# Linear attention, a token-and-channel mixer and a normalised channel mixer on one core: weight loads placed earlier, second weights decoded in the second mixing, and the last sums of the first mixing taken between the first products of the second

## The chip, the cores and the metric

The kernel runs on one core of one Trainium2 chip. The metric is device time in microseconds (us) of one execution. TensorE (PE) multiplies, VectorE (DVE), ScalarE (ACT) and GpSimd (POOL) do elementwise work, and SyncE (SP) issues almost all DMAs. Every engine takes its own instructions in order; SP's DMAs of this kernel all stand in one queue, and a DMA there that waits for a buffer holds those behind it.

## The reference

Three steps, in float32 from weights given as float64, B = 8 batches of S = 576 tokens, 512 channels:

```
q_s = exp(q - max_d q) / sum_d;   k_s = exp(k - max_s k) / sum_s        # 8 heads of 64
x   = q_s @ (k_s^T @ v)                                                 # linear attention
u   = x + (relu(x^T @ w_tok1) @ w_tok2)^T                               # token mixing, 576 -> 256 -> 576
x   = u + relu(u @ w_ch1) @ w_ch2                                       # first channel mixing, 512 -> 1536 -> 512
xn  = (x - mean) / sqrt(var + 1e-6) * g_ln
out = x + relu(xn @ w2_ch1) @ w2_ch2                                    # second channel mixing, 512 -> 2048 -> 512
```

## The kernel before

**Precision.** Each float32 operand of a matmul is a pair, a high part in the reduced format `fp32r` and the rest. Three matmuls (`PASSES`) make one product. ACT makes the high part and DVE or POOL the low one: `split`, and `relu_split` (L155 on ACT, L156 on DVE) for hidden values. A weight comes as 64 bits an element and is *decoded* by five operations (`decode`): rebias (L113 on ACT, or L111 on DVE where the decode is of the "late" form), shift (L119), sign (L126), low (L132 in the usual form), all DVE, and the splitting into parts (ACT L148 and POOL L150, or L140 and L141 in the late form).

**First channel mixing** (`Phase1`). The tokens are nine blocks of 512 columns; block 8 holds the leftover tokens of all batches. A block has twelve steps f. A step issues L1 (twelve 128x512 matmuls into `ph`, L707), the relu and split of the result into `h`, and L2 of the step two before (`LAG`; twelve 128x512 matmuls into four banks `acc`, L724). At a block's end `finish` adds the residual into `yT` (L745 on DVE, and L748 on POOL for the low part), `y_store` transposes `yT` (`py`, L659), takes the statistics (L670, L671) and stores rows. Work of other kinds is laid between the matmuls in two ways. `tick()` is called four times a step and runs what `later(n, ...)` put n ticks ahead. `work(7)` stands after L1 and after L2 and takes seven entries from a list `jobs`, so that a step takes fourteen.

**Preparing the second mixing**, in blocks 7 and 8. Its first product is done with Strassen-Winograd's seven products of 2x2 blocks. `combine_all` prepares the first weights (`w2_ch1`) in eight groups g: two loads of 512 KB into `stage` tiles (L835), decode, sums (L860), seven splits (ACT L886, POOL L891), three stores to `wc_dram` (L897). `w2_jobs` does the second weights (`w2_ch2`) in 16 chunks of 512 KB (load L1028): six of them into `stage` tiles in block 8, the other ten, in pairs, into parts of `yb` in the second mixing, decoded in the late form. `Root` computes the inverse deviation, turns it (`pm`, L794) and stores it. The normalised first tokens are made in place in `xs` by POOL's hats (L1098: subtract, multiply), ACT's gains, POOL's differences (L1113) and splits into seven operands `xc` (L1107, L1108).

**Second mixing.** Six sets of 768 tokens, eight passes q each (48 in all). A pass has seven products i (L1213, six 128x384 matmuls into one of two banks `pp`, in turn), each followed by `gather` (DVE L1226 and `relu_split`), and six `token_chunk`s of the pass before (L1251, six 128x512). `ring_load` (L1067) fetches the combined weights of pass q + 2 after products 3 and 6. `at(q, i, ...)` hangs work behind a product; `work(2)` takes two entries of `jobs` after each product from q = 1 on.

The order of all instructions is this written order; there is no scheduler. What the change moves is in `Combine.splitting`, `combine_all`, `w2_jobs`, `Root.start`, the loop over steps, the list of `at(...)` ahead of the passes, and `work` in the loop over passes.

## Time and profile before

| | |
|---|---|
| median of 3 runs | 1662.68 us (1662.41 to 1667.33) |
| the profiled execution | 1666.4 us |
| its span, first to last instruction | 1664.6 us |
| PE busy | 1599.8 us, 96% |
| DVE busy | 794.7 us, 48% |
| ACT busy | 494.6 us, 30% |
| POOL busy | 495.7 us, 30% |

The profile is of one execution, and 1.8 us of it lie outside the span. Busy times overlap; for a bound one asks which engine the others wait for, and where. A row of a timeline gives the start of a group of like instructions, how long the group took, the engine, the line of the kernel, the operation, output and inputs with their shapes, and in brackets the idle time before it with what ended it.

### The profile page before, as it was taken

Reading aid. Unit: us, or ns where it says so; the run is one execution under the profiler, and the core shown is the slowest. Engines: PE = TensorE matmul, PEld = TensorE weight load, DVE = VectorE, ACT = ScalarE, POOL = GpSimd, SP = SyncE. Lnnn points to the kernel's source line nnn. Section 1 sums busy time; section 2 is a strip of 40 time slices with the busy share of each in tenths; the row PEclk is TensorE's granted clock in tenths of the full one; section 3 lists DMA queues with packets and bytes.
Section 4 is the critical chain, followed back from the end, with each engine's and each line's share of the span. In section 5 each row is a group of like instructions: output and inputs, shape, how many; then the busy total and the mean of one; then the engine's idle time right before and its main releaser. Section 6 shows DMA issues by size and latency. Waiting matters only on the chain. (4 is left out here: it accounts for less than half of the span.)

```text
span 1664.6 us, 21709 instructions
## 1 busy us (share of the span) xinstructions
PE 1599.8 (96%) x8241; PEld 1401.3 (84%) x8241; DVE 794.7 (48%) x1551; ACT 494.6 (30%) x1022; POOL 495.7 (30%) x412
## 2 busy tenths in 40 slices
PE   5999999999999999999878899999999999999998
PEld 4888888888888888877757789889889989998997
DVE  7775535344443435355645555335335335335333
ACT  5663323333232323333332223122122122122111
POOL 5744612232222314233652350320320320320001
PEclk8999999999999999999989999999999999999999
DMA  8552313122121313047754545544544544544341
GB/s 218 143 164 81 116 41 95 43 78 58 42 88 38 99 35 94 22 165 272 295 204 153 178 169 186 173 167 146 173 168 145 171 171 143 173 171 139 121 171 38
DMA packets 154398, 222.58 MB, mean 134 GB/s; under 512 B 97918, under 2 KB 114102, under 8 KB 146102
## 3 DMA queue, kind: packets, MB, share of 16 engines
q1 hardware_dynamic: 145750, 202.02, 37.9%
q10 hardware_dynamic: 5600, 9.73, 1.6%
q0 software_dynamic: 2944, 9.44, 1.6%
q8 instruction: 65, 1.06, 0.3%
q14 instruction: 39, 0.32, 0.1%
HBM read 174.98 MB, written 46.17 MB: 133 GB/s over the span
## 5 line engine op out<-in xcount | busy, mean ns | idle before, releaser
L1213 PE MATMUL pp<-xc,wr 128*128 128x384 f32 x2016 | 398.2, 340 | 15.3 <-DVE h L156 8.0
L1213 PEld LDWEIGHTS pp<-xc,wr 128*128 128x128 f32 x2016 | 362.6, 189 | 36.5 <-DVE h L156 9.5
L707 PE MATMUL ph<-u,w 128*128 128x512 f32 x1296 | 327.3, 398 | 11.3 <-DVE h L156 11.3
L724 PE MATMUL acc<-h,w 128*128 128x512 f32 x1296 | 329.0, 399 | 4.6 <-DVE yT L745 4.6
L1251 PE MATMUL acc<-w,h 128*128 128x512 f32 x1152 | 289.8, 393 | 0.0
L707 PEld LDWEIGHTS ph<-u,w 128*128 128x128 f32 x1296 | 238.7, 190 | 59.8 <-DVE h L156 12.2
L724 PEld LDWEIGHTS acc<-h,w 128*128 128x128 f32 x1296 | 240.9, 191 | 53.5 <-ACT wc L886 5.0
L1251 PEld LDWEIGHTS acc<-w,h 128*128 128x128 f32 x1152 | 214.4, 188 | 38.8
L155 ACT ACTIVATE h<-sc 128x384 fp32r<-128x384 f32 x144 | 75.6, 525 | 329.5 <-DVE sc L1226 327.0
L1251 PE MATMUL acca<-w,h 128*128 128x512 f32 x576 | 148.3, 394 | 0.0
L156 DVE SCALAR_TENSOR_TENSOR h<-ph,h 128x512 fp32r<-128x512 f32 x108 | 74.0, 686 | 144.8 <-ACT h L155 144.5
L156 DVE SCALAR_TENSOR_TENSOR h<-sc,h 128x384 fp32r<-128x384 f32 x144 | 90.1, 626 | 94.3 <-ACT h L155 94.3
L1098 POOL TENSOR_TENSOR xs<-xs 128x768 f32<-128x768 f32 x48 | 89.4, 1887 | 144.8 <-DMA xs<-mr_dram 144.8
L1267 POOL DMA_DIRECT2D out<-yb x32 | 17.7, 553 | 361.3 <-DVE yb L1263 361.2
L1251 PEld LDWEIGHTS acca<-w,h 128*128 128x128 f32 x576 | 107.8, 189 | 16.7
L1226 DVE TENSOR_TENSOR sc<-su,pp 128x384 f32<-128x384 f32 x144 | 79.5, 552 | 60.8 <-PE pp L1213 59.9
L155 ACT ACTIVATE h<-ph 128x512 fp32r<-128x512 f32 x108 | 64.2, 594 | 142.3 <-PE ph L707 140.9
L1226 DVE TENSOR_TENSOR su<-su,pp 128x384 f32<-128x384 f32 x96 | 53.0, 552 | 104.3 <-PE pp L1213 104.1
L486 POOL TENSOR_TENSOR qt<-rawq,qm 128x640 f32<-128x640 f32 x24 | 30.3, 1261 | 228.3 <-PE pt L480 130.6
L156 DVE SCALAR_TENSOR_TENSOR h<-pp,h 128x384 fp32r<-128x384 f32 x48 | 26.7, 556 | 144.1 <-ACT h L155 144.1
L155 ACT ACTIVATE h<-pp 128x384 fp32r<-128x384 f32 x48 | 23.6, 491 | 241.6 <-PE pp L1213 241.6
L629 PE MATMUL pu<-w,hs 128*128 128x288 f32 x384 | 61.8, 296 | 0.1
(178 smaller groups left out, 1740.5 us busy)
## 6 DMA issues: line engine op xcount, KB each, us to landing
wr<-wc_dram SPq DMA_DIRECT2D x48, 1024.0 KB, 5.1
wr<-wc_dram SPq DMA_DIRECT2D x48, 768.0 KB, 4.4
st<-in_moe_w_ch SPq DMA_DIRECT2D x23, 512.0 KB, 4.8
yT_dram<-yT SPq DMA_DIRECT2D x9, 1024.0 KB, 5.0
vt<-in_v SPq DMA_DIRECT2D x64, 128.0 KB, 3.1
y_dram<-yn ACTq DMA_DIRECT2D x32, 256.0 KB, 2.6
wc_dram<-wc SPq DMA_DIRECT2D x16, 512.0 KB, 3.2
out<-yb POOLq DMA_DIRECT2D x32, 256.0 KB, 2.8
```

The source lines that it names most:

```text
L155: nc.scalar.activation(out=hi, in_=x, func=AF.Relu)
L156: nc.vector.scalar_tensor_tensor(out=lo, in0=x, scalar=0.0, in1=hi.bitcast(F32), op0=ALU.max, op1=ALU.subtract)
L486: nc.gpsimd.tensor_tensor(out=self.qt, in0=self.qr.rearrange("p h c d -> p c h d"), in1=self.qm.unsqueeze(3).to_broadcast([P, NC + 1, 2, D ...
L629: nc.tensor.matmul(out=pu[:, 0:HN], lhsT=l, rhs=r, start=(n == 0), stop=(n == len(terms) - 1))
L707: nc.tensor.matmul(out=ps, lhsT=w[:, x, kk, fo:fo + P], rhs=u[:, y, kk], start=(n == 0), stop=(n == 3 * KD - 1),)
L724: nc.tensor.matmul(out=self.acc[dd], lhsT=w[:, x, f % 2, dd * P:(dd + 1) * P], rhs=h[:, y], start=(f == self.f0 and n == 0), stop=(f == se ...
L1098: nc.gpsimd.tensor_tensor(out=y, in0=y, in1=m, op=(ALU.subtract, ALU.mult)[op])
L1213: nc.tensor.matmul(out=bank[(BANK[i] + q) % 2][:, 0:HT], lhsT=r[:, x, kk], rhs=xc[i][:, y, kk], start=(n == 0 and not add), stop=(n == 5), ...
L1226: nc.vector.tensor_tensor(out=o, in0=x, in1=y, op=ALU.add)
L1251: nc.tensor.matmul(out=acc[c], lhsT=h[:, x, m * P:(m + 1) * P], rhs=wb2[p][:, y, f], start=(p == 0 and n == 0), stop=(p == NP - 1 and n == 5),
L1267: nc.gpsimd.dma_start(out=dst, in_=y)
```

## The change

- In `Combine.splitting` the three splits that need no sum come first. `combine_all` loads the first two groups at once, waits 20 empty entries, and issues the load of group g + 1 among the splits of group g - 1, at the sixth place. Splits and decoding alternate one to one.
- `Root` turns and stores two and three ticks later.
- `w2_jobs` goes by single chunks with a `depth` of loads ahead and a `gap` of empty entries. Only chunks 0 and 1 are done in block 8. Chunks 2 and 3 are loaded into the upper half of `xs` behind the first product and decoded in the late form; chunks 4 to 15 go through four parts of `yb` from product (1,1) on, with three loads ahead. `work` takes two entries a product in pass 0 and three afterwards.
- The four ring loads of passes 0 and 1 are spread over ticks 6 to 18 of step 6.
- The last step of block 8 does no L2. The three L2s that are left stand after products 0 and 1 and, in halves, after 3 and 4; the sums into `yT` follow product 4, POOL's additions products 5 to 8, and the `y_store`s the first four of pass 1. The tiles that are taken over (`acc`, `yb`, `acca`, `h11`) are taken later by as much.

```diff
-            for n, fn in zip((0, 2, 6, 8), (self.root, self.rstd, self.turn, self.store)):
+            for n, fn in zip((0, 2, 8, 11), (self.root, self.rstd, self.turn, self.store)):
...
-            ops += part(A11, 0) + part(s[:, 0], 1) + part(A12, 2) + [store(0, 3)]
+            ops += part(A11, 0) + part(A12, 2) + part(A22, 6)
+            ops += part(s[:, 0], 1) + [store(0, 3)]
             ops += part(s[:, 1:3], 3, 2) + [store(3, 2)]
-            ops += part(s[:, 3], 5) + part(A22, 6) + [store(5, 2)]
+            ops += part(s[:, 3], 5) + [store(5, 2)]
...
+                if 0 < g < NP - 1:
+                    f.insert(6, cs[g + 1].load)
                 ops = []
                 while f or d[:-4]:
-                    ops += f[0:2]
-                    del f[0:2]
+                    if f:
+                        ops.append(f.pop(0))
                     if len(d) > 4:
                         ops.append(d.pop(0))
-                ops += [cs[g + 1].load] if g + 1 < NP else []
...
-            jobs.extend(todo + [lambda: expand(0)])
+            jobs.extend([cs[0].load, cs[1].load] + [nop] * 20 + [lambda: expand(0)])
...
+        def w2_jobs(chunks, stages, depth, ts=None, gap=12):
...
+                if not ts:
+                    ops = [ops[0], lambda x=ops: [x[k]() for k in (1, 2, 3)], nop, ops[4]]
+                jobs[0:0] = ops
+
+            out = [lambda n=n: load(n) for n in chunks[:depth]] + [nop] * gap
+            for k, n in enumerate(chunks):
+                out.append(lambda n=n: go(n))
+                if k + depth < len(chunks):
+                    m = chunks[k + depth]
+                    out.append(lambda m=m: load(m))
             return out
...
-                    later(8, lambda: [ring_load(n, x) for n in range(2) for x in range(2)])
+                    later(6, lambda: ring_load(0, 0))
+                    later(9, lambda: ring_load(0, 1))
+                    later(14, lambda: ring_load(1, 0))
+                    later(18, lambda: ring_load(1, 1))
...
-                    jobs += w2_jobs(range(0, 3), lambda i: stage(512))
+                    jobs += w2_jobs([0, 1], lambda n: stage(512), 2)
...
-            if len(pend) > LAG:
+            if len(pend) > LAG and not (o.j == B and f == NF1 - 1):
                 do_L2()
...
         def last_rows():
+            do_L2(nop, range(2, KD))
             tmp["add"] = lastp.finish()
...
-        at(0, 0, lambda: do_L2(nop))
+        at(0, 0, lambda: jobs.extend(w2_jobs([2, 3], flat64, 2, ts, 6)))
...
+        at(0, 0, lambda: [do_L2(nop), h_tile(("11", 0))])
         at(0, 1, lambda: do_L2(nop))
-        at(0, 2, last_rows)
+        at(0, 2, lambda: h_tile("22"))
+        at(0, 3, lambda: pend[0][0].L2(*pend[0][1:], nop, range(2)))
+        at(0, 4, last_rows)
+        for c, (q, i) in enumerate(((0, 5), (0, 6), (1, 0), (1, 1))):
+            at(q, i, lambda c=c: tmp["add"](c))
+        at(1, 1, lambda: nc.sync.dma_start(out=yT_dram[B], in_=yT_t[B]))
         for c in range(CT):
-            at(0, 3 + c, lambda c=c: tmp["add"](c))
-        at(0, 6, lambda: nc.sync.dma_start(out=yT_dram[B], in_=yT_t[B]))
-        for c, (q, i) in enumerate(((0, 5), (0, 6), (1, 0), (1, 1))):
-            at(q, i, lambda c=c: y_store(B, c))
+            at(1, c, lambda c=c: y_store(B, c))
...
+            jobs.extend(w2_jobs([*range(4, NF2)], flat64, 3, ts, 0))
...
-        at(0, 6, take_over)
-        at(1, 1, more_acc)
+        at(0, 6, take_banks)
+        at(1, 1, take_over)
+        at(1, 3, more_acc)
+        at(2, 6, other_h)
...
-                if q and jobs:
-                    work(2)
+                work(2 + (q > 0))
```

How instructions stand on SP's queue while the weights are combined (loads L835 into the tiles `st` and `stage`, stores L897 of a group's results), before:

```order
L835 DMA st<-in_moe_w_ch 128x2x512 x2
L835 DMA stage_6662<-in_moe_w_ch 128x2x512
L835 DMA stage_6663<-in_moe_w_ch 128x2x512
L897 DMA wc_dram<-wc 128x1536
L897 DMA wc_dram<-wc 128x1024 x2
```

and after:

```order
L835 DMA stage_6662<-in_moe_w_ch 128x2x512
L835 DMA stage_6663<-in_moe_w_ch 128x2x512
L754 DMA yT_dram<-yT 128x2048
L835 DMA st<-in_moe_w_ch 128x2x512 x2
L897 DMA wc_dram<-wc 128x1536
```

The loads of the third group have moved ahead of the first group's stores, and so on for the later groups.

SP's queue from the end of block 8 to the second pass (L1028 chunks of the second weights, L1067 ring loads `wr`, L1300 the last store of `yT`), before:

```order
L1028 DMA st<-in_moe_w_ch 128x1024 x3
L1067 DMA wr<-wc_dram 128x2048
L1067 DMA wr<-wc_dram 128x1536
L1067 DMA wr<-wc_dram 128x2048
L1067 DMA wr<-wc_dram 128x1536
L1028 DMA st<-in_moe_w_ch 128x1024 x3
L1067 DMA wr<-wc_dram 128x2048
L1300 DMA yT_dram<-yT 128x2048
L1067 DMA wr<-wc_dram 128x1536
L1028 DMA yb<-in_moe_w_ch 128x1024 x2
```

and after (the same, as L1027, L1057 and L1305):

```order
L1027 DMA st<-in_moe_w_ch 128x1024 x2
L1057 DMA wr<-wc_dram 128x2048
L1057 DMA wr<-wc_dram 128x1536
L1057 DMA wr<-wc_dram 128x2048
L1057 DMA wr<-wc_dram 128x1536
L1027 DMA xs<-in_moe_w_ch 128x1024 x2
L1057 DMA wr<-wc_dram 128x2048
L1057 DMA wr<-wc_dram 128x1536
L1305 DMA yT_dram<-yT 128x2048
L1027 DMA yb<-in_moe_w_ch 128x1024 x3
```

Two chunk loads instead of three stand ahead of the four ring loads and two instead of three behind them, now into `xs`; the first loads into `yb` are three and stand behind the store of `yT`, as before.

DVE's queue in the first seven products (L1226 and L1220 the gathers, L745 the last sums of the first mixing, L111 to L126 the decode of a chunk), before:

```order
L156 SCALAR_TENSOR_TENSOR h_7874<-pp,h_7874 128x384
L745 TENSOR_TENSOR yT<-acc_7391,u 128x512
L745 TENSOR_TENSOR yT<-acc_7392,u 128x512
L745 TENSOR_TENSOR yT<-acc_7393,u 128x512
L745 TENSOR_TENSOR yT<-acc_7394,u 128x512
L1226 TENSOR_TENSOR su<-su,pp 128x384
L1226 TENSOR_TENSOR sc<-su,pp 128x384
L156 SCALAR_TENSOR_TENSOR h_7928<-sc,h_7928 128x384
```

and after:

```order
L1220 TENSOR_TENSOR sc<-su,pp 128x384
L156 SCALAR_TENSOR_TENSOR hh<-sc,hh 128x384
L745 TENSOR_TENSOR yT<-acc_7367,u 128x512
L745 TENSOR_TENSOR yT<-acc_7368,u 128x512
L745 TENSOR_TENSOR yT<-acc_7369,u 128x512
L745 TENSOR_TENSOR yT<-acc_7370,u 128x512
L111 TENSOR_SCALAR xs<-xs 128x512
L1220 TENSOR_TENSOR sc<-su,pp 128x384
L156 SCALAR_TENSOR_TENSOR h_7825<-sc,h_7825 128x384
L119 TENSOR_SCALAR sd<-xs 128x512
```

The four sums stood behind the third product's gather and now stand behind the fifth's, with the first operation of chunk 2 after them and ahead of the sixth's.

## Rows read from the trace of the kernel before

**Rows 1.** The page's forty slices: TensorE's busy share, in tenths.

```profile
PE   5999999999999999999878899999999999999998
```

**Rows 2.** Windows: stretch, length, busy PE, PEld, DVE, ACT, POOL; clock; DMA.

```profile
744.63:810.37 65.74, 56.98 (x234) 46.00 (x233) 39.92 (x71) 25.30 (x56) 27.12 (x32) 0.92 0.76 280
847.70:886.96 39.26, 25.63 (x97) 20.31 (x96) 20.10 (x24) 14.78 (x24) 19.38 (x11) 0.83 0.38 148
886.96:909.31 22.35, 20.19 (x101) 18.00 (x100) 12.78 (x26) 5.22 (x10) 5.68 (x4) 0.92 0.63 223
922.87:933.66 10.79, 5.60 (x20) 4.80 (x19) 6.73 (x12) 0.73 (x2) 5.53 (x3) 0.68 0.49 182
938.19:942.89 4.70, 2.69 (x13) 2.08 (x13) 3.98 (x5) 1.10 (x3) 2.81 (x2) 1.00 0.96 338
962.40:971.28 8.88, 5.24 (x20) 4.64 (x20) 7.57 (x11) 1.61 (x3) 4.38 (x3) 0.81 0.14 33
984.85:1000.53 15.68, 15.68 (x80) 14.13 (x78) 8.09 (x12) 3.60 (x7) 10.74 (x6) 1.00 0.35 118
```

**Rows 3.** PE's timeline where nothing waits: start, length, engine, line, operation, names.

```profile
718.70 2.88 PE L707 MATMUL ph<-u,w 128*128 128x512 f32 x12
721.42 2.88 PE L724 MATMUL acc<-h,w 128*128 128x512 f32 x12
...
988.33 1.21 PE L1213 MATMUL pp<-xc,wr 128*128 128x384 f32 x6
989.38 1.54 PE L1251 MATMUL acca<-w,h 128*128 128x512 f32 x6
```

**Rows 4.** PE's timeline, two waits in A and B.

```profile
805.12 5.46 PE L724 MATMUL acc<-h,w 128*128 128x512 f32 x12 [4.58 <-DVE yT L745]
...
867.63 4.99 PE L707 MATMUL ph<-u,w 128*128 128x512 f32 x12 [9.94 <-DVE h L156]
```

**Rows 5.** ACT's timeline: the first step of a decode, in A and B.

```profile
745.02 0.66 ACT L113 ACTIVATE st<-st 128x512 f32<-128x512 f32 x1 [5.20 <-DMA st<-in_moe_w_ch]
...
861.76 0.65 ACT L113 ACTIVATE st<-st 128x512 f32<-128x512 f32 x1 [9.89 <-DMA st<-in_moe_w_ch]
```

**Rows 6.** SP's timeline in B.

```profile
848.02 1.82 SPq L1067 DMA_DIRECT2D wr<-wc_dram  x4
...
850.51 16.58 SPq L1028 DMA_DIRECT2D st<-in_moe_w_ch  x3
```

**Rows 7.** POOL's groups, 815 to 990: count, busy us, mean ns, idle before.

```profile
L1098 POOL TENSOR_TENSOR xs<-xs 128x768 f32<-128x768 f32 x16 | 30.0, 1892 | 30.6 <-DMA xs<-mr_dram 30.6
...
L1113 POOL TENSOR_TENSOR xs<-xs 128x768 f32<-128x768 f32 x4 | 8.7, 2165 | 0.2
L150 POOL TENSOR_TENSOR w<-st,w 128x512 fp32r<-128x512 f32 x6 | 7.8, 1306 | 13.2 <-ACT w L148 13.2
```

**Rows 8.** DVE's timeline in C, D, E and F.

```profile
889.21 2.47 DVE L745 TENSOR_TENSOR yT<-acc,u 128x512 f32<-128x512 f32 x4
...
925.92 0.90 DVE L111 TENSOR_SCALAR yb<-yb 128x512 f32<-128x512 f32 x1 [7.44 <-DMA yb<-in_moe_w_ch]
...
939.29 1.74 DVE L786 TENSOR_SCALAR r<-r 128x8 f32<-128x8 f32 x1
...
942.99 0.43 DVE L111 TENSOR_SCALAR yb<-yb 128x512 f32<-128x512 f32 x1
...
962.06 1.84 DVE L111 TENSOR_SCALAR yb<-yb 128x512 f32<-128x512 f32 x1 [5.03 <-DMA yb<-in_moe_w_ch]
```

**Rows 9.** DMA issues, 740 to 980: count, KB each, median us to landing.

```profile
st<-in_moe_w_ch SPq DMA_DIRECT2D x11, 512.0 KB, 4.9
...
yb<-in_moe_w_ch SPq DMA_DIRECT2D x10, 512.0 KB, 8.4
```

**Rows 10.** Window of the tile `yb` alone (ten decodes): busy DVE, ACT, POOL.

```profile
900.00:990.00 90.00, 25.29 (x40) 5.99 (x10) 13.65 (x10) 0.94 0.57 198
```

**Rows 11.** SP's waits over the whole span: total us, times, longest.

```profile
SPq L1067 <- PE pp L1213: 665.3, 91, 22.1
```

More of the change, by code (lines that the diff above doesn't have):

```diff
@@ L712, in L1, with L2 @@
             return ps, BLK
-        def L2(self, f, h, mid):
-            if f == self.f0:
+        def L2(self, f, h, mid, dds):
+            if f == self.f0 and not dds[0]:
                 self.acc = [
@@ L719, in L2 @@
             w = wb[f // 2]
-            for dd in range(KD):
+            for dd in dds:
                 if dd == KD // 2:
@@ L977, with do_L2 @@
             steps += [(o, f) for f in range(o.f0, o.f1)]
-        def do_L2(mid=tick):
+        def do_L2(mid=tick, dds=range(KD)):
             o, f, h = pend.pop(0)
@@ L996, in combine_all @@
             cs = [Combine(g) for g in range(NP)]
-            todo = [cs[0].load]
-            late = []
             def expand(g):
@@ L1014, in expand @@
                 jobs[0:0] = ops
-            jobs.extend(todo + [lambda: expand(0)])
-        def w2_job(g, stages, ts=None):
-            box = {}
-            def load(i):
-                def fn():
-                    if i == 0:
-                        wb2[g] = main.tile([P, 2, 2, DM], F32R, tag="w", bufs=NF1, name="w")
-                    st = box[i] = stages(i)
-                    f0 = (2 * g + i) * P
-                    nc.sync.dma_start(
-                        out=st.rearrange("p d t -> p (d t)"), in_=w2_ch2[f0:f0 + P, :]
-                    )
-                return fn
-            def go():
-                both = [
-                    decode(box[i], lambda x: x, wb2[g][:, 0, i], wb2[g][:, 1, i], ts and ts[i])
-                    for i in range(2)
-                ]
-                if ts:
-                    jobs[0:0] = [x for pair in zip(*both) for x in pair]
-                    return
-                ops = [b[0] for b in both]
-                for b in both:
-                    ops += [lambda b=b: [b[n]() for n in (1, 2, 3)], nop, nop]
-                jobs[0:0] = ops + [b[4] for b in both]
-            return [load(0), load(1)], go
@@ L1048, in w2_jobs, with load, go @@
-        def w2_jobs(gs, stages, ts=None):
-            made = [w2_job(g, stages, ts) for g in gs]
-            out = list(made[0][0])
-            for n, (_, go) in enumerate(made):
-                out.append(go)
-                if n + 1 < len(made):
-                    out += made[n + 1][0]
+            jobs.extend([cs[0].load, cs[1].load] + [nop] * 20 + [lambda: expand(0)])
+        def w2_jobs(chunks, stages, depth, ts=None, gap=12):
+            st = {}
+            def load(n):
+                g, i = n // 2, n % 2
+                if i == 0:
+                    wb2[g] = main.tile([P, 2, 2, DM], F32R, tag="w", bufs=NF1, name="w")
+                st[n] = stages(n)
+                nc.sync.dma_start(
+                    out=st[n].rearrange("p d t -> p (d t)"), in_=w2_ch2[n * P:(n + 1) * P, :]
+                )
+            def go(n):
+                ops = decode(
+                    st[n], lambda x: x, wb2[n // 2][:, 0, n % 2], wb2[n // 2][:, 1, n % 2],
+                    ts and ts[n % 2],
+                )
+                if not ts:
[7 more added lines that the diff above has]
+                    out.append(lambda m=m: load(m))
@@ L1294, with flat64 @@
         lastp = steps[-1][0]
-        at(0, 0, lambda: do_L2(nop))
-        at(0, 1, lambda: do_L2(nop))
-        at(0, 2, last_rows)
+        sts = [xs[0][:, i * 1024:(i + 1) * 1024] for i in (2, 3)]
+        ts = [sd[:, i * 512:(i + 1) * 512].bitcast(U32) for i in range(2)]
+        at(0, 0, lambda: jobs.extend(w2_jobs([2, 3], flat64, 2, ts, 6)))
+        def flat64(n):
+            return sts[n % len(sts)].bitcast(U32).rearrange("p (n t) -> p n t", t=2)
+        at(0, 0, lambda: [do_L2(nop), h_tile(("11", 0))])
@@ L1301, with take_banks @@
[L1301 to L1302 removed]
+            at(1, c, lambda c=c: y_store(B, c))
+        def take_banks():
+            for i, c in enumerate((3, 4, 5, 0)):
+                acc[c] = ps_acc.tile([P, 512], F32, tag=f"acc{i}", name=f"acc{i}")
         def take_over():
[L1305 to L1324 removed]
@@ L1326, in more_acc @@
+            y = main.tile([P, 4096], F32, tag="u", bufs=2, name="yb")
+            yb.append(y)
+            tmp["t2"] = y[:, CS * DM:CS * DM + 2 * HT].rearrange("p (k n) -> p k n", k=2)
+            sts[:] = [y[:, i * 1024:(i + 1) * 1024] for i in range(4)]
+            jobs.extend(w2_jobs([*range(4, NF2)], flat64, 3, ts, 0))
         def more_acc():
```

32 lines of the change are left out of this document (8 added, 24 removed).

## The prediction

> **What bounds the kernel now.** I read four kinds of view, from coarse to fine. First the forty slices of the page [rows 1]: TensorE (PE) is busy nine tenths and more of almost every slice; only the first one, the last one and four about the middle (the 20th to the 23rd, 791 to 957 us) are lower. So the span is PE's own work nearly everywhere, and a change that takes nothing off PE can gain only where PE waits. Next the stretches of that dip, as PE's waits cut them [rows 2]; I call them A to F in the order of those rows, and the last row is a steady pass of the second mixing. Then PE's timeline at full rate [rows 3]: twelve 128x512 matmuls follow one another after 721.42 - 718.70 = 2.72 us, six 128x384 after 989.38 - 988.33 = 1.05 us; so six of 512 columns are 1.36. A lone small product of 128 columns I put at 0.09, an estimate from 2.72/12 = 0.227 for 512 columns with its hand-over.
>
> With these each stretch has a full-rate length, and what is above it is loss (waits, and the lower granted clock that follows them):
> - A, 228 matmuls of 512 = 19 x 2.72 = 51.7, some six small ones 0.4: 52.1 of 65.74, loss 13.6.
> - B, 7 x 2.72 + 2 x 1.05 = 21.1 of 39.26, loss 18.1.
> - C, ten products 10.5, four token chunks 5.4, sixteen transposes 1.4: 17.3 of 22.35, loss 5.0.
> - D and F, each two products and one token chunk, 3.5: of 10.79 and 8.88, losses 7.3 and 5.4.
> - E, one product and one chunk, 2.4 of 4.70, loss 2.3.
>
> Together 51.7 us, 3.1% of the span. The granted clock stood at 0.68 to 0.92 of full speed in A to D and F, at 1.00 in E and the steady pass [rows 2].
>
> Who is late there: in A and B the chain begins at DMA. ScalarE (ACT) is in order; its L113, the first step of decoding a weight, waited 5.20 us for a load, and 9.89 in the worst place [rows 5]. Behind it in ACT's queue stand the relus (L155) without which VectorE (DVE) cannot finish `h`, and PE stood 9.94 us for `h` [rows 4]. The 9.89 has its reason on SP: four ring loads were issued at 848.02, the third to fifth chunk from 850.51 behind them [rows 6]. In D and F it is DVE's own L111 that waits for chunks in `yb`, 7.44 and 5.03 us [rows 8], with the gathers behind it.
>
> **The change part by part.** No matmul is added or removed, so each part is costed as what is left of the losses.
>
> *Combining loads (A).* Seventeen entries of `jobs` instead of seven now lie between a load and its first use. Fourteen entries go with one step of two groups, 5.44 us, so ten more are 3.9 us: a lead of about 6.6 against a landing of 4.9 [rows 9]. ACT should stop waiting; the cover is 1.7 us and a load that lands late gives the difference back. The stall of 4.58 on `yT` [rows 4] came as DVE stood behind ACT, so it should go as well. The transpose `pm` is two ticks later, hence after `mr`. The twenty empty entries put the combining 20/14 = 1.4 steps later; the jobs of chunks 0 and 1 stand behind it in the same list, so that they can only come later. Left: 1 (0 to 5; the upper end if half the landings still outrun the lead).
>
> *End of block 8 (B).* The two remaining chunk loads stand ahead of all ring loads on SP, and these are spread over twelve ticks: the cause of the 9.89 is gone. What is late next is GpSimd (POOL). It has still, in its order, the last group's splits, four hats of 1.89, two chunk splits of 1.31 and four diffs of 2.17 [rows 7]; and the chunk loads stand in SP's queue behind the last store of combined weights, which waits for POOL's last split of a group. Chain from there: landing 4.9, two decodes at the 2.53 of the nearest row [rows 10] 5.1, two splits 2.6, four diffs 8.7 and one hat between them 1.9 come to 23.2; PE has 7 x 2.72 + 1.05 = 20.1 of work before it needs the last operand, so it is some 3 late, and 4 with the clock. Left: 4 (1 to 10; the ends are the whole chain hidden, and chunk loads that land after 8.4 as `yb`'s do [rows 9], plus a hat).
>
> *First seven products (C).* The pending L2s of 9, 10 and 11 now fill gaps between products, the same 36 matmuls. DVE's four last sums L745 (2.47 together, [rows 8]) and L111 now stand ahead of the gathers of products five and six; PE has two banks, so the product of the next pass waits for most of that: 2 to 3 us. The new late decode of chunks 2 and 3 is on DVE here too, 2 x 2.5 us [rows 10]. Its loads have the span of three products and two L2s, 8.6 us, against 4.9 to 8.4. Left: 4.5 (2 to 7).
>
> *Chunk 4 onward (D).* Its load cannot start before POOL's last addition L748, since the buffer is the old `u`; it stands behind the store of `yT` on SP, and the decode follows one product later in `jobs`. From the first product of the stage: three L2s and five products 13.4, sums 2.5, four additions at POOL's 1.31 for tiles of that size [rows 7] 5.2, landing 8.4: 29.5 us. DVE gets there with the tenth product, by PE's rate and C's loss after 27 to 28. It waits some 2, the rest is clock. Left: 4 (1 to 8; the upper end is the old wait).
>
> *Rstd (E).* L784 to L786 are still issued while POOL does hats: 1.74 us for 128x8 [rows 8]. Left: 2 (0 to 4).
>
> *Later chunks (F).* The loads stand three ahead; one chunk is taken up in 7 entries, three per pass, so the lead is about 15 us against 8.4. But SP is one queue: a chunk load stands behind ring loads that wait for products (665.3 us in 91 waits, 7.3 each, the longest 22.1 [rows 11]) and the x load. Left: 2 (0 to 6).
>
> *Denser decode (G), new.* Twelve chunks instead of ten lie in the second mixing, and three per pass rather than two: 3 x 2.53 = 7.6 us of DVE per pass [rows 10] on top of the 8.09 of a steady pass, 15.7 of 15.68 at worst [rows 2], though a part of the 2.53 is itself time beside POOL. Before, the fewer chunks lost nothing outside D to F. Left: 4 (0 to 10; the ends are decode wholly in gaps and each of twelve chunks giving back 0.8 us).
>
> Sum: 1 + 4 + 4.5 + 4 + 2 + 2 + 4 = 21.5 left of 51.7, a gain of 30.2. The profiled execution, 1666.4 around a span of 1664.6, would be 1636; it is 0.2% above the median of the runs, 1662.68, and from that the forecast is 1662.7 - 30.2 = **1632.5 us**, with 1624 to 1643 for it alone (every term half a step off).
>
> **A rule against this change.** L111 took 0.43 us at 942.99 and 1.84 at 962.06 while a hat of POOL's ran; the 128x8 operation of E took 1.74, also beside a hat [rows 8]. The Trainium skill, SBUF — State Buffer, section "SBUF: two separate sides", says that the port pair that VectorE and GpSimd share is an exclusive lock: an instruction of either that needs it holds it to its end, and the other is fully blocked. The trace agrees in that the excess of L111, 1.4 us, is under one hat. By that rule more decoding on DVE while POOL has hats, subtractions and diffs makes each collision cost up to a POOL instruction, and the gain would be smaller; that is the second rival, which I work out from the rows.
>
> **The rivals.**
> 1. *Nearly every stall goes* (A 0, B 2, C 2, D 2, the rest 1 each): 9 left, gain 42.7, **1620**. For it: each named wait is on a load, and each load is earlier. [...]
> 2. *DVE becomes the bound in passes one to four*: twelve chunks that each meet a hat or a subtraction lose 1.4, some 17 us; as gatherings stand behind them PE sees most: G 10, D 8, E 4, F 5, with A, B and C as forecast 36.5 left, gain 15, **1647**. For it: 7.6 + 8.09 fills a pass. Against: DVE's queue may run ahead into the two banks' slack.
> 3. *The change doesn't do what it says*: the landings stretch as more loads are in flight, ACT's L113 waits on as before (A 13.6, B 10), the rest as forecast: 40 left, gain 12, **1651**. For it: the 4.9 is a median, and `yb`'s 8.4 shows what traffic does.
> 4. *Slower*: SP's queue. Chunk loads 7 to 15 are issued with no lead, because ring loads ahead of them wait for products, and DVE's L111 waits a whole landing, 8.4, for each of nine chunks: 75.6 instead of F's 2. That is 44 above before, **1706**. It decides from a mean wait of 30.2/9 + 0.2 = 3.6 us per chunk. For it: the longest wait of 22.1 is more than a lead of 15. Against: these loads stand between ring loads whose products are near.
>
> **How the numbers follow.** Chances: forecast 0.57, first rival 0.13, second 0.13, third 0.07, slower by SP's queue 0.05, and 0.05 for several of these in part that end within 0.3% (5 us, about what a measurement of this kernel can tell from no change). Faster is 0.57 + 0.13 + 0.13 + 0.07 = 0.90, same 0.05, slower 0.05. The range takes in the forecast and the second rival, 1618 to 1652; it leaves out the better half of the first rival, the two last cases and a little of the third, some 0.2.
>
> **What would show it.** Right: no L113 of 3 us or more on DMA in blocks 7 and 8; no gap near 10 before L707 at the end of block 8, and a late POOL diff as the releaser of what is left; the first product of the second pass released by DVE behind L745; one L111 wait of 2 to 3 us for chunk 4 and none after; steady passes of 15.7. Wrong: L113 waits that stay (third rival); L111 or L119 of 1.5 us and more all through passes one to four with PE released by DVE (second); repeated L111 waits on `yb` loads (fourth); or a loss in a stretch that lost nothing before.

## The result, and the profile after

The changed kernel takes **1647.05 us** (median of 4 runs, 1645.75 to 1647.95). Against the kernel before, run beside it (1664.92), the ratio is 0.9892 with a 95% interval of 0.9871 to 0.9913: about 18 us faster. The forecast was 1632.5, so the sign and the range held, and little more than half of the forecast gain came. The profiled execution has a span of 1645.5 us against 1664.6, 19.1 less.

The page's forty slices of the kernel after, TensorE's busy share in tenths (it answers [rows 1]):

```profile
PE   5999999999999999999998799999999999999998
```

Of the four low slices two are left, 864 to 946 us. Windows of the kernel after, in the order of [rows 2] and with the same columns: from a step of block 8 to product (0,5), the next eleven products, then old D, old E, the stretch between, old F:

```profile
836.33:867.16 30.83, 26.79 (x115) 21.99 (x114) 17.49 (x18) 11.55 (x19) 14.39 (x8) 0.94 0.51 195
867.16:898.93 31.77, 27.25 (x137) 23.21 (x136) 25.55 (x45) 8.35 (x16) 9.96 (x8) 1.00 0.59 205
898.93:904.84 5.91, 5.91 (x31) 5.41 (x30) 4.22 (x6) 1.34 (x3) 2.15 (x2) 1.00 0.87 335
904.84:924.77 19.93, 13.30 (x49) 11.07 (x48) 15.99 (x23) 3.62 (x7) 10.23 (x6) 0.83 0.57 200
924.77:933.11 8.34, 8.34 (x44) 7.59 (x42) 5.68 (x10) 3.16 (x6) 1.29 (x1) 1.00 0.42 50
933.11:952.03 18.92, 15.28 (x67) 13.13 (x66) 14.32 (x18) 4.61 (x9) 11.43 (x7) 0.91 0.76 266
```

The third and the fifth row have PE busy from end to end; all that is lost lies in the others. Where PE waits, on its timeline (it answers [rows 4]; the last bracket is the wait and its releaser):

```profile
800.37 0.63 PE L659 MATMUL py<-ident,yT 128*128 128x128 f32 x4 [1.20 <-DVE st L132]
847.48 4.61 PE L707 MATMUL ph<-u,w 128*128 128x512 f32 x12 [2.84 <-DVE h L156]
...
871.00 1.33 PE L1207 MATMUL pp<-xc,wr 128*128 128x384 f32 x6 [1.57 <-DVE sc L1220]
...
885.79 1.32 PE L1207 MATMUL pp<-xc,wr 128*128 128x384 f32 x6 [1.99 <-DVE hw L156]
...
909.77 1.33 PE L1207 MATMUL pp<-xc,wr 128*128 128x384 f32 x6 [2.35 <-DVE sc L1220]
912.78 2.29 PE L1207 MATMUL pp<-xc,wr 128*128 128x384 f32 x6 [1.68 <-DVE sc L1220]
919.44 2.29 PE L1207 MATMUL pp<-xc,wr 128*128 128x384 f32 x6 [2.61 <-DVE sc L1220]
939.69 2.29 PE L1207 MATMUL pp<-xc,wr 128*128 128x384 f32 x6 [2.91 <-DVE sc L1220]
```

The 4.58 and the 9.94 of before are gone. In their place stand eight waits of 1 to 3 us, most of them for a gather (`sc`) on VectorE. A row of 2.29 is the same six matmuls at the lower clock level (the granted clock is 0.50 from 912.80 to 914.80), a row of 1.33 at the upper (1.00 from 909.80 to 911.10). The lower level did not come after every wait: it followed the 1.68 us at 912.78, not the 2.35 at 909.77 just before.

To compare the stretches I set the start of the same product in both traces side by side. The loss of before is that of the prediction, but B is cut from C at product 5, so that 2.1 us of C's 5.0 stand with B.

| stretch | lost before | forecast left | left after | how |
|---|---|---|---|---|
| A | 13.6 | 1 | 2.5 | 11.1 us gained by the step with the first `py` of block 8 |
| B, to product 5 (892.20, now 867.16) | 20.2 | 4 + a part of C | 6.5 | 25.0 us ahead there, 13.7 more than at A's end |
| products 5 to 16 (920.45, now 898.93) | 2.9 | the rest of C's 4.5 | 6.4 | 21.5 ahead |
| D, to product 19 | 7.3 | 4 | 0 | 28.8 ahead |
| E, to product 24 | 2.3 | 2 | 10.2 | 20.9 ahead |
| F, to product 33 | 5.4 | 2 | 5.7 | 20.6 ahead |
| G, to product 44 | 0 | 4 | 1.5 | 19.1 ahead, as at the end |

51.7 lost before, 21.5 forecast, 32.8 measured. At product 19 the kernel was 28.8 us ahead, almost the whole forecast; then E, F and G took 9.7 back.

What VectorE did in E and F, on its timeline (it answers [rows 8]), and GpSimd's rows beside it:

```profile
906.34 0.97 DVE L111 TENSOR_SCALAR yb<-yb 128x512 f32<-128x512 f32 x1 [2.41 <-DMA yb<-in_moe_w_ch]
907.42 1.84 DVE L119 TENSOR_SCALAR sd<-yb 128x512 uint32<-128x512 uint32 x1
909.18 0.54 DVE L1220 TENSOR_TENSOR sc<-su,pp 128x384 f32<-128x384 f32 x1
...
914.84 1.57 DVE L784 TENSOR_TENSOR r<-mr 128x8 f32<-128x8 f32 x1
916.44 1.73 DVE L785 TENSOR_TENSOR r<-r,ve 128x8 f32<-128x8 f32 x1
918.21 0.17 DVE L786 TENSOR_SCALAR r<-r 128x8 f32<-128x8 f32 x1
...
938.22 0.95 DVE L111 TENSOR_SCALAR yb<-yb 128x512 f32<-128x512 f32 x1 [2.98 <-DMA yb<-in_moe_w_ch]
...
940.28 2.21 DVE L156 SCALAR_TENSOR_TENSOR hh<-sc,hh 128x384 fp32r<-128x384 f32 x1 [0.65 <-ACT hh L155]
942.42 2.06 DVE L119 TENSOR_SCALAR sd<-yb 128x512 uint32<-128x512 uint32 x1
```

```profile
905.19 3.79 POOL L1088 TENSOR_TENSOR xs<-xs 128x768 f32<-128x768 f32 x2 [1.28 <-DMA xs<-mr_dram]
913.00 1.28 POOL L141 TENSOR_TENSOR w<-sd,w 128x512 fp32r<-128x512 f32 x1 [4.02 <-ACT w L140]
914.24 3.92 POOL L1088 TENSOR_TENSOR xs<-xs 128x768 f32<-128x768 f32 x2
...
940.26 3.93 POOL L1088 TENSOR_TENSOR xs<-xs 128x768 f32<-128x768 f32 x2
```

Two explanations offer themselves. One is SP's queue: chunk 7 was waited for 2.41 us, and in F chunk 11 for 2.98, as their loads stand behind the x load and the scatter of `mr`. The other is VectorE beside GpSimd: L784 and L785 handle 8 numbers a partition and take 1.57 and 1.73 us while two hats run from 914.24 to 918.16; L786, just behind them, takes 0.17. In F the same shows in L156 and L119, 2.21 and 2.06 us. I call these two the queue and the contention (or density) theory. The experiments tell these apart.

### The profile page after: what moved, and what is told of

The parts are those of the page before. It is cut to its first block, busy times and chain, and to the rows that moved or that the text cites. A ratio compares the mean times of both kernels' runs of the same rounds, so it can differ in the third digit from the quotient of the medians.

```text
span 1645.5 us, 21697 instructions
## 1 busy us (share of the span) xinstructions
PE 1595.0 (97%) x8241; PEld 1395.8 (85%) x8241; DVE 819.1 (50%) x1555; ACT 492.0 (30%) x1018; POOL 498.5 (30%) x412
## 4 chain that ended last, share of the span: by engine, by line
PE 83%; DVE 5%; DMA 4%; POOL 3%; issue 2%; ACT 2%; SPq 1%; POOLq 0%; ACTq 0%; DVEq 0%
PE pp L1207 19%; PE ph L707 16%; PE acc L724 15%; PE acc L1245 15%; PE acca L1245 7%; PE pu L629 4%; PE pg L568 3%; PE pk L538 2%; DMA yb<-in_moe_w_ch 2%; PE pq L589 1%; PE py L659 1%; POOL wc L891 1%; PE pq L614 1%; DMA xs<-mr_dram 1%; DVE sd L119 1%
## 5 line engine op out<-in xcount | busy, mean ns | idle before, releaser
L1207 PEld LDWEIGHTS pp<-xc,wr 128*128 128x128 f32 x2016 | 361.1, 189 | 39.7 <-DVE sc L1220 15.4
L707 PE MATMUL ph<-u,w 128*128 128x512 f32 x1296 | 326.3, 397 | 2.9 <-DVE h L156 2.8
L724 PE MATMUL acc<-h,w 128*128 128x512 f32 x1296 | 323.9, 395 | 0.0
L707 PEld LDWEIGHTS ph<-u,w 128*128 128x128 f32 x1296 | 238.0, 189 | 50.7 <-DVE h L156 3.3
L724 PEld LDWEIGHTS acc<-h,w 128*128 128x128 f32 x1296 | 237.2, 188 | 47.3
L1245 PE MATMUL acc<-w,hh 128*128 128x512 f32 x648 | 180.5, 393 | 0.0
L1245 PE MATMUL acc<-w,h 128*128 128x512 f32 x501 | 145.5, 398 | 0.4 <-DVE h L156 0.4
L1245 PEld LDWEIGHTS acc<-w,hh 128*128 128x128 f32 x648 | 121.6, 188 | 26.6
L156 DVE SCALAR_TENSOR_TENSOR h<-ph,h 128x512 fp32r<-128x512 f32 x108 | 74.1, 687 | 138.1 <-ACT h L155 137.9
L155 ACT ACTIVATE hh<-sc 128x384 fp32r<-128x384 f32 x96 | 50.5, 526 | 249.8 <-DVE sc L1220 247.3
L1245 PE MATMUL acca<-w,hh 128*128 128x512 f32 x432 | 114.2, 391 | 0.0
L1220 DVE TENSOR_TENSOR sc<-su,pp 128x384 f32<-128x384 f32 x144 | 79.5, 552 | 61.5 <-PE pp L1207 60.7
L1245 PEld LDWEIGHTS acc<-w,h 128*128 128x128 f32 x501 | 93.9, 190 | 13.5 <-DVE h L156 1.3
L1220 DVE TENSOR_TENSOR su<-su,pp 128x384 f32<-128x384 f32 x96 | 53.1, 553 | 102.4 <-PE pp L1207 102.2
L156 DVE SCALAR_TENSOR_TENSOR hh<-sc,hh 128x384 fp32r<-128x384 f32 x96 | 63.4, 661 | 63.0 <-ACT hh L155 63.0
L1245 PEld LDWEIGHTS acca<-w,hh 128*128 128x128 f32 x432 | 80.5, 188 | 14.0
```

The source lines that it names most:

```text
L155: nc.scalar.activation(out=hi, in_=x, func=AF.Relu)
L156: nc.vector.scalar_tensor_tensor(out=lo, in0=x, scalar=0.0, in1=hi.bitcast(F32), op0=ALU.max, op1=ALU.subtract)
L707: nc.tensor.matmul(out=ps, lhsT=w[:, x, kk, fo:fo + P], rhs=u[:, y, kk], start=(n == 0), stop=(n == 3 * KD - 1),)
L724: nc.tensor.matmul(out=self.acc[dd], lhsT=w[:, x, f % 2, dd * P:(dd + 1) * P], rhs=h[:, y], start=(f == self.f0 and n == 0), stop=(f == se ...
L1207: nc.tensor.matmul(out=bank[(BANK[i] + q) % 2][:, 0:HT], lhsT=r[:, x, kk], rhs=xc[i][:, y, kk], start=(n == 0 and not add), stop=(n == 5), ...
L1220: nc.vector.tensor_tensor(out=o, in0=x, in1=y, op=ALU.add)
```

## Experiments

All start from the kernel after. Times are medians of four runs; 1647.05 is the number to compare with, and the ratio is to the kernel before, which ran beside each batch and came to 1662.84 to 1664.92. The interval of a ratio is 0.0015 to 0.0021 (2.5 to 3.5 us) to either side, and by the ratios most gains come out 1 or 2 us smaller than by the medians; so a difference of 2 or 3 us between two of these kernels is not shown by the times alone. Where the text says how far ahead a kernel is at a product, two traces are compared, one execution each.

### The scatter later

```diff
-        at(3, 0, root.scatter)
+        at(12, 0, root.scatter)
```

> The kernel after, with only the scatter of the last rows' statistics (mr to mr_dram, two DMAs of 4-byte elements) moved from behind product (3,0) to behind product (12,0). Theory queue: in the kernel after chunks 11 and 12 were issued at 920.29 behind this scatter, which waited for rstd until 918.41 and then kept the DMA engines busy at 2 to 11 GB/s; L111 of chunk 11 waited 2.98 us and PE lost 5.8 us between 933.11 and 952.03. Without it those chunks are issued some 7 us earlier, L111 does not wait, and 4 to 6 us go: about 1642. Theory density (VectorE is too full beside GpSimd's hats, whatever the loads do): the L119 of 2.06 and the L156 of 2.21 beside hats stay, at most 1.5 us go: 1645.5 to 1647.

**1645.04 us** (1642.92 to 1647.48), ratio 0.9887 (0.9869 to 0.9904). Not clear of the kernel after, and nearer to the second theory. F's DMA wait did go, but PE lost there again, on other waits for VectorE:

```profile
936.06 1.32 PE L1207 MATMUL pp<-xc,wr 128*128 128x384 f32 x6 [1.85 <-DVE sc L1220]
...
940.49 1.32 PE L1207 MATMUL pp<-xc,wr 128*128 128x384 f32 x6 [1.24 <-DVE sc L1220]
```

### The whole root later

```diff
-        at(2, 3, root.root)
-        at(2, 5, root.rstd)
-        at(3, 0, root.scatter)
+        at(12, 0, root.root)
+        at(12, 2, root.rstd)
+        at(13, 0, root.scatter)
```

> The kernel after, with the whole root of the last rows (L775 to L789, and the scatter) moved to passes 12 and 13, where no weight is decoded. Theory queue with small operations: beside what the scatter gives, the L784 and L785 of 1.57 and 1.73 us beside hats no longer stand ahead of the sum that product (3,1) waits for: 2.61 us of waiting and the 1.1 us of low clock behind it go as well: 7 to 10 us, about 1638.5. Theory density: only the 3.7 us of VectorE's own root operations go from this stretch, 2 to 4 us: about 1644.

**1641.60 us** (1640.55 to 1642.17), ratio 0.9865: 5.4 us faster, between the two. Of these, 1.1 were there already at product 19, ahead of the edit. L111's wait for chunk 7 grew to 3.67 us.

### Four chunk loads ahead

```diff
-            jobs.extend(w2_jobs([*range(4, NF2)], flat64, 3, ts, 0))
+            jobs.extend(w2_jobs([*range(4, NF2)], flat64, 4, ts, 0))
```

> The kernel after, with four chunk loads ahead instead of three, so that the load of chunk 7 stands ahead of the x load on SP (that one waited until 892.58 for the store of y). Theory queue: L111's wait of 2.41 us at 903.9 goes, and with it the 2.35 and part of the 1.68 us of PE behind it and some low clock: 3 to 5 us, about 1643; the chunks behind the scatter stay as they are. Theory density: the wait is only filled by the next late operation, under 1.5 us: 1645.5 to 1647.

**1642.57 us** (1641.21 to 1644.47), ratio 0.9872: 4.5 us faster. Taken alone it speaks for the queue. But the load of chunk 7 had moved by one place only (issued at 893.76 instead of 895.52, still behind the x load), and L111 waited 1.45 us, 1 less.

### Both together

The two edits above at once.

> The kernel after, with the whole root in passes 12 and 13 and chunk loads four ahead, the two edits that alone gave 1641.6 and 1642.6. If they remove different losses (VectorE's root operations and the scatter; the wait for chunk 7), they add up: some 9 to 10 us below the kernel after, about 1637.5. If both only shorten the same queue of VectorE behind chunk 7's wait, the second adds 1 to 2 us: about 1640.5.

**1644.69 us** (1641.50 to 1645.83), ratio 0.9880: 2.4 us faster than the kernel after and by the median worse than either edit alone (the ranges overlap). Neither case of the expectation allowed that. In the traces it is 3.2 us ahead at the end, the two alone 5.6 and 5.1. VectorE's timeline, and GpSimd's beside it, show why:

```profile
905.38 2.08 DVE L119 TENSOR_SCALAR sd<-yb 128x512 uint32<-128x512 uint32 x1
907.49 2.17 DVE L126 SCALAR_TENSOR_TENSOR sd<-yb,sd 128x512 uint32<-128x512 uint32 x1
909.70 2.17 DVE L132 SCALAR_TENSOR_TENSOR sd<-yb,sd 128x512 uint32<-128x512 uint32 x1
911.80 0.54 DVE L1220 TENSOR_TENSOR sc<-su,pp 128x384 f32<-128x384 f32 x1
```

```profile
905.22 6.11 POOL L1088 TENSOR_TENSOR xs<-xs 128x768 f32<-128x768 f32 x3 [1.78 <-DMA wr<-wc_dram]
```

Three hats run back to back, and three operations of a decode take one hat's length each: 6.4 us for what takes 0.43 + 0.69 + 0.69 = 1.8 elsewhere. The gather behind them waits, and PE stood 5.11 us for it; a second such place cost 3.84. Whichever edit moves the decode of a chunk moves it into or out of a hat. So the gains of the runs so far are partly luck of position.

### No hats

```diff
-                for n in range(4):
-                    at(q0 + 2, 3 + n, lambda n=n: hat(n % 2, 0, n // 2))
+                for n in range(4 if s else 0):
+                    at(q0 + 2, 3 + n, lambda n=n: hat(n % 2, 0, n // 2))
...
-                for n in range(4):
-                    at(q0 + 3, 3 + n, lambda n=n: hat(n % 2, 1, n // 2))
+                for n in range(4 if s else 0):
+                    at(q0 + 3, 3 + n, lambda n=n: hat(n % 2, 1, n // 2))
```

> The kernel after, without GpSimd's eight hats (L1088) for the second token set, so that this set's tokens go in unnormalised; all loads stay. Theory contention (operations of VectorE beside a hat take 1.3 to 2.2 us instead of 0.2 to 0.7): the L119, L156, L784 and L785 that were long beside hats go back to their short times, some 9 us of VectorE between 904 and 943, of which PE sees 6 to 9: about 1639.5. Theory queue (the two waits of L111 for chunks, 2.41 and 2.98 us, are the cause and the rest follows them): these waits stay, 1 to 3 us faster: about 1645.

This kernel leaves out the normalising of the second token set, so it only shows what the eight hats cost.

**1635.94 us** (1635.21 to 1638.05), ratio 0.9832 (0.9816 to 0.9849): 11 us faster, more than either theory said. Windows of E and F in this run:

```profile
905.30:919.24 13.94, 10.84 (x50) 8.43 (x49) 9.71 (x22) 3.43 (x7) 1.53 (x2) 1.00 0.84 286
927.57:941.51 13.94, 13.76 (x68) 11.82 (x66) 11.63 (x19) 4.73 (x9) 3.88 (x3) 1.00 0.89 345
```

E's products take 13.94 instead of 19.93 us, F's 13.94 instead of 18.92, at the full clock. VectorE's rows say where it went, and what was not the cause:

```profile
907.12 0.43 DVE L111 TENSOR_SCALAR yb<-yb 128x512 f32<-128x512 f32 x1 [2.73 <-DMA yb<-in_moe_w_ch]
...
L785 DVE TENSOR_TENSOR r<-r,ve 128x8 f32<-128x8 f32 x1 | 0.2, 168 | 0.0
```

L785 takes 0.17 us instead of 1.73. The wait for chunk 7 is still there, 2.73 us, and longer than before; the product behind it then waits 0.71 for VectorE, where it waited 2.35. Nor did VectorE wait for GpSimd's results: in the kernel after, none of its rows in E and F has GpSimd as a releaser. So the contention is the larger cause by far. What is left in E without the hats, 13.94 us where 9.7 would lose nothing (19.93 less the 10.2), is 4.2 us, the most that the queue's wait can cost there by itself.

### Hats behind the decoding

The numbers are products from the set's first pass on; `put(k, fn)` hangs `fn` behind the k-th.

```diff
+                h0, g0, l1, h1, g1, df = (17, 22, 21, 24, 30, 42)
+                if s == 0:
+                    h0, g0, l1, h1, g1, df = (33, 38, 37, 40, 43, 45)
...
-                    at(q0 + 2, 3 + n, lambda n=n: hat(n % 2, 0, n // 2))
+                    put(h0 + n, lambda n=n: hat(n % 2, 0, n // 2))
...
```

> The kernel after, computing everything, with the eight hats of the second token set moved from passes 2 and 3 to products (4,5) to (6,1), behind nearly all late decoding (the load of the rows in between, the gains and diffs moved by as much as they must). Theory contention: like the kernel without these hats, which gave 1635.9, less what the hats now cost at their new place, where gathers read PSUM and only the relu's low part reads SBUF: 7 to 10 us faster than the kernel after, about 1638.5. Theory that hats cost the same wherever they stand (DMA or GpSimd's own chain, splits of xc late in pass 7): within 2 us of 1647.

**1639.40 us** (1638.53 to 1641.24), ratio 0.9860 (0.9843 to 0.9876): 7.7 us faster, with all work done. E and F again have their short length (this kernel is 12.9 us ahead of the kernel after at product 33), and what is paid at the new place shows in the third window, of products (4,5) to (5,2), behind which it is 8.7 ahead:

```profile
904.09:916.86 12.77, 10.51 (x49) 8.50 (x48) 9.69 (x22) 3.12 (x6) 1.51 (x2) 1.00 0.89 290
925.19:939.13 13.94, 13.73 (x67) 11.81 (x66) 11.64 (x19) 3.71 (x7) 3.88 (x3) 1.00 0.74 279
939.13:956.87 17.74, 14.36 (x61) 11.95 (x60) 14.68 (x17) 3.67 (x8) 10.02 (x6) 0.90 0.24 87
```

There the last chunks are still being decoded, and L111 and L119 take 2.05 and 1.84 us beside a hat.

### The combining as before

```diff
-            ops += part(A11, 0) + part(A12, 2) + part(A22, 6)
-            ops += part(s[:, 0], 1) + [store(0, 3)]
+            ops += part(A11, 0) + part(s[:, 0], 1) + part(A12, 2) + [store(0, 3)]
...
-                if 0 < g < NP - 1:
-                    f.insert(6, cs[g + 1].load)
...
+                ops += [cs[g + 1].load] if g + 1 < NP else []
                 ops += d
...
-            jobs.extend([cs[0].load, cs[1].load] + [nop] * 20 + [lambda: expand(0)])
+            jobs.extend([cs[0].load, lambda: expand(0)])
```

> The kernel after, with the combining of the first weights as before (load of the next group just ahead of its decoding, no 20 empty entries, old order of splits); the rest of the change stays. Theory load lead: ScalarE's L113 waits 4 to 5 us for loads again, PE stands for py, acc and ph in blocks 7 and 8, and the 11.6 us that stretch A gained (13.6 lost before, 2.0 after) come back: about 1658. Rival (A's gain came from the later root, or from the two blocks' other work): under 3 us slower.

**1651.23 us** (1649.78 to 1652.97), ratio 0.9922: only 4.2 us slower. ScalarE waits as it did, and so does PE:

```profile
744.00 0.67 ACT L113 ACTIVATE st<-st 128x512 f32<-128x512 f32 x1 [5.20 <-DMA st<-in_moe_w_ch]
...
797.19 0.66 ACT L113 ACTIVATE st<-st 128x512 f32<-128x512 f32 x1 [4.94 <-DMA st<-in_moe_w_ch]
```

```profile
803.65 5.46 PE L724 MATMUL acc<-h,w 128*128 128x512 f32 x12 [5.54 <-DVE yT L745]
```

In block 8's step 10 this kernel is 10.1 us behind the kernel after (L707 at 849.10 against 839.05), as A's gain wants. At product (0,0) it is only 5.3 behind (857.65 against 852.33), since the 2.84 us of waiting at 847.48, and the 1.7 that the row there takes above its 2.88 at full rate, do not occur in it. So the earlier loads gain some 10 us, and the end of block 8 takes back nearly half, because what it waits for does not come earlier by as much.

### Eight empty entries instead of twenty

```diff
-            jobs.extend([cs[0].load, cs[1].load] + [nop] * 20 + [lambda: expand(0)])
+            jobs.extend([cs[0].load, cs[1].load] + [nop] * 8 + [lambda: expand(0)])
```

> The kernel after, with 8 empty entries instead of 20 ahead of the first decode of the combining, all load leads of later groups as they are; everything behind it in the list ends 12 entries, 4.7 us, earlier against PE. Theory chain: with the combining as before, block 8's end came 10.1 us later on PE's clock but product (0,0) only 5.3 later, so 4.7 us of A's gain are lost in B because GpSimd's and ScalarE's list ends later; here 3 to 4.5 us come back: about 1643. Rival (what is late in B is the hats' and diffs' own place, given in ticks): the time stays within 1.5 us of 1647, or is higher by a wait for the first group's load.

**1646.05 us** (1645.55 to 1646.20): the rival's case. The wait at L707 shrank to 1.70, but product (0,0) then stood 1.84 for `h`, and it started 1.6 us earlier, not 3 to 4.5.

### Longer gap ahead of the last chunks

```diff
-                    jobs += w2_jobs([0, 1], lambda n: stage(512), 2)
+                    jobs += w2_jobs([0, 1], lambda n: stage(512), 2, None, 30)
```

> The kernel after, with 30 empty entries instead of 12 between the loads of chunks 0 and 1 and their decoding in block 8. In the kernel after ScalarE's L113 waited 5.53 us for chunk 0, GpSimd's two splits L150 of these chunks stood ahead of its four diffs L1103, and PE lost some 6.5 us between 844.5 and 861.25. Here three of the four diffs stand ahead of the splits. Theory GpSimd chain: the diffs end some 6 us earlier and 3 to 5 us go: about 1643. Rival (the diffs are not what is late, but the relu behind ScalarE's L148): the decode only meets PE later, and the time stays within 1.5 us, or rises, as the decode's end comes nearer to the first token chunk.

**1646.63 us** (1643.39 to 1647.45): no change. L707 did not wait any more, but product (0,0) did, and some low clock followed:

```profile
851.18 1.94 PE L1207 MATMUL pp<-xc,wr 128*128 128x384 f32 x6 [3.19 <-DVE h L156]
```

### Ring loads together again

```diff
-                    later(6, lambda: ring_load(0, 0))
-                    later(9, lambda: ring_load(0, 1))
-                    later(14, lambda: ring_load(1, 0))
-                    later(18, lambda: ring_load(1, 1))
+                    later(8, lambda: [ring_load(n, x) for n in range(2) for x in range(2)])
```

> The kernel after, with the four ring loads of passes 0 and 1 issued together eight ticks into step 6 as before, the two chunk loads of block 8 in their new number and places. In the kernel before the wait of 9.89 us for a chunk load arose behind these four; now only chunks 0 and 1 are decoded in block 8. Theory order: if the lot still stands behind both chunk loads on SP, spreading has no part in the gain and the time is within 1.5 us of 1647. Rival (the lot gets ahead of the chunk loads, or fills the DMA engines while they land): L113 waits some 8 to 10 us in block 8 and 5 to 9 us come back, about 1653.

**1646.98 us** (1646.05 to 1648.05): no change. Both chunk loads stand ahead of the lot either way, and SP issues it together either way: at 833.47 here, at 833.87 in the kernel after. Of the two things that ended the 9.89 us of [rows 5], it was the number and place of the chunks, not the spread.

### The last L2s in their old places

```diff
-            if len(pend) > LAG and not (o.j == B and f == NF1 - 1):
+            if len(pend) > LAG:
...
         def last_rows():
-            do_L2(nop, range(2, KD))
...
+        at(0, 2, last_rows)
         at(0, 2, lambda: h_tile("22"))
-        at(0, 3, lambda: pend[0][0].L2(*pend[0][1:], nop, range(2)))
-        at(0, 4, last_rows)
```

> The kernel after, with the last three L2s of block 8 placed as before: step 9's in block 8, the other two whole behind products (0,0) and (0,1), and the sums L745 behind (0,2); the additions, y_stores and chunk loads keep the places of the kernel after. Theory cover: products (0,1) to (0,4) wait for the operands that GpSimd's four diffs (9.35 us) make late, and the moved L2s were filling that; 2 to 5 us slower, about 1650.5. Rival (the place of L745 ahead of the sixth gather costs as much as the cover brings): within 1.5 us of 1647, or faster.

**1644.91 us** (1643.43 to 1645.94): the rival's case, by the medians 2 us faster, which the times alone do not show (1645.75 to 1647.95 for the kernel after). In the trace it is 0.8 us ahead at product 5 and 2.4 at product 19. With the sums L745 two products earlier, one wait of 1.53 us stands where the kernel after has 1.57 and 0.62.

### Hats apart, old L2s, eight entries

Three of the edits above at once.

> The kernel after with three edits: the hats of the second set behind the decoding, the L2s of block 8 in their old places, 8 empty entries instead of 20. If the three act on different stretches (E and F, C, B), their gains add: 8.5 + 2 + 4 to about 1633. If B's gain and that of the L2s are the same time (either covers GpSimd's diffs), about 1636.5.

**1635.77 us** (1634.79 to 1637.59), ratio 0.9835 (0.9821 to 0.9850): the fastest with all work done, 11 us below the kernel after. It lies nearer to the second case: the edits at block 8's end do not add in full.

## Why the prediction was right, and where not

**What bounds, and A.** Right. PE's own work sets nearly all of the span, and the waits began at loads. With the loads earlier, L113's longest wait for a load in A is 0.69 us (5.20 before), and A gained 11.1 us of the 12.6 forecast. What the sum did not have is that B does not move with it (the combining put back costs 4.2, not 11.6).

**B and C.** With the first five products B left 6.5 us, and the eleven behind them 6.4: together 12.9 against 8.5. L113's wait in block 8 stayed, which I had taken for gone (5.53 us, where less than 3 was to be the sign of being right): SP issued the two chunk loads only at 831.53, behind a store of combined weights (L897, 828.46) that waits for GpSimd, as the sum itself had it.

```profile
837.22 0.68 ACT L113 ACTIVATE st<-st 128x512 f32<-128x512 f32 x1 [5.53 <-DMA st<-in_moe_w_ch]
...
844.55 0.66 ACT L148 ACTIVATE w<-st 128x512 fp32r<-128x512 f32 x1 [2.21 <-DVE st L132]
```

The relu that PE wants at 844.5 stands behind that L148. I named GpSimd as what is late next; its diffs do run from 846.54 to 855.89. But freeing one (a longer gap, fewer empty entries) let the other take its place. What would free both was not found, and that part stays open. One candidate stands in VectorE's rows: four L1098 (the low parts of the operands) beside the diffs took 1.65 to 2.43 us each, the fifth, with GpSimd idle, 0.94; no run tests what that costs. In C the wait behind L745 came in its place (1.57 us, forecast 2 to 3). The 0.62 and the 1.99 later are not L745's: they stand behind the decodes of chunks 2 and 3, whose L119 took 1.52 and 1.39 us beside GpSimd's additions (L748), a meeting that the term did not have. The moved L2s, meant to fill gaps, show no gain: put back, the kernel is no slower.

**D.** Better than forecast, 0 left instead of 4. The load of chunk 4 was issued at 881.63 and L111 took it at 887.75 without a wait: a landing of at most 6.1 us, not 8.4. The rest of the chain was off by the same 8 us on both sides: counted from product (0,0), the load went out after 29.3 us instead of 21.1, and VectorE came to it after 35.4 instead of 27 to 28. So the wait is missing because of the shorter landing, and that both sides moved alike is luck.

**E, F and G.** Here the step failed. I gave them 2, 2 and 4 us and they took 10.2, 5.7 and 1.5. E's term had only the small operations of the root beside hats, F's only loads, G's VectorE's sum of work; a decode or a low part held by a hat, with a gather behind it that PE waits for, was priced only in a rival. The rows that could have told me are in [rows 8], L111's 0.43 and 1.84, and L786's 1.74. The experiments show it on the kernel itself: 11 us without eight hats, 7.7 with them put elsewhere.

How long VectorE is held does not decide alone. Summed over its operations that stood beside these eight hats, the length above what the same operation takes alone is 6.1 us in the kernel before (five operations) and 8.7 in the kernel after (seven); it is 8.3 and 9.5 in the runs with the later root and with four loads ahead (eight each), which are 5 us faster than the kernel after all the same. I take it that what counts is whether a gather that PE waits for stands next; no run separates this.

**The rivals.** The second rival gave 1647 and the kernel takes 1647.05. It named the right mechanism (decode beside GpSimd's hats, gathers behind it), and the wrong places: it put 8 us into D, where the kernel after has no hat, and spread its price over twelve chunks, while the 11 us that go with the hats go in E and F alone. That the times agree is chance: it had 27 for D to G, where 17.4 are left, and 9.5 for A to C, where 15.4 are. The first rival (9 us left) falls with the eight waits. The third (loads do not help) falls with A and D, though the L113 wait in block 8 that it named did stay; the fourth with L111's two waits of 2.41 and 2.98, 5.4 us in all, where it needed 3.6 for each of nine chunks, though the median landing of `yb` loads did rise from 8.4 ([rows 9]) to 12.1:

```profile
yb<-in_moe_w_ch SPq DMA_DIRECT2D x12, 512.0 KB, 12.1
```

So the first-choice time was 14.5 us too low, and the range held because it had been taken out to the second rival. The signs say the same: no wait for chunk 4 but two for later chunks, and L119s of 1.84 and 2.06 us with PE behind VectorE, the sign given for the second rival.

## What to carry to other kernels

When a change moves work to an engine that has room by its busy share, look at which instructions of another engine stand beside it, one by one: an operation that takes four times as long in some rows of the trace than in others says that time depends on a neighbour, and packing more in multiplies those meetings. A load that is made early gains only what the next late thing allows, so undo each part alone before it is credited. Two edits that each gain by shifting work a little can lose together; take the neighbour away once, and the size of its share is known.

## What the runs showed of the hardware

While an operation of GpSimd runs, an operation of VectorE that is held beside it ends only behind it, and each holds one. In the run with both edits three operations took 2.08, 2.17 and 2.17 us beside three hats of 6.11 us in all; a 128x8 operation is held as long as a 128x512 one (1.73 and 1.84). Only operations whose operands are all in SBUF were held. The gather, which adds a PSUM bank to an SBUF operand, kept its time, as the run with the hats behind the decoding shows; L156 ahead of it, with both inputs in SBUF, did not (0.56 alone):

```profile
962.96 2.12 DVE L156 SCALAR_TENSOR_TENSOR h<-sc,h 128x384 fp32r<-128x384 f32 x1 [0.65 <-ACT h L155]
...
965.00 0.54 DVE L1220 TENSOR_TENSOR sc<-su,pp 128x384 f32<-128x384 f32 x1
```

```profile
962.81 7.92 POOL L1088 TENSOR_TENSOR xs<-xs 128x768 f32<-128x768 f32 x4 [3.57 <-DMA xs<-mr_dram]
```

The same L156 reading PSUM is not held either: in the kernel after, `h<-ph,h` at 846.74 took 0.69 us, its usual time, while GpSimd's diffs ran from 846.54.

This is the rule of the Trainium skill, SBUF — State Buffer, section "Who interferes with whom": a VectorE instruction with two SBUF inputs contends with a GpSimd instruction that reads SBUF, one in a mode that uses both port pairs contends with GpSimd too, and the one that comes later is fully blocked. The traces agree in the rows named: L126, L132, L784, L785 and L156 on `sc` have two inputs in SBUF and were held, L1220 and L156 on `ph` have one and were not. L111 and L119 have a single one and were held too (1.84 to 2.08 us); by that page this means a two-port mode, which no run here shows by itself.

The scatter of `mr` is 4 KB a DMA, two of them, and took 13.1 us to land, longer than a ring load of 1 MB (median 9.7 us from 800 to 980, in the same trace); in the two microseconds from 925 on the DMA engines moved 11 GB/s:

```profile
mr_dram<-mr SPq DMA_DIRECT2D x2, 4.0 KB, 13.1
```

```profile
925.00:927.00 2.00, 2.00 (x12) 1.79 (x11) 0.88 (x2) 0.98 (x2) 0.00 (x0) 1.00 0.05 11
```

The engines were busy 0.05 of that time, so they were not full, and yet the load of chunk 11, issued from 920.29 on behind the scatter, was only there at 938.2. What held it was not looked into; moving the scatter away gave 2 us at most.
